# Moving copies, scatters and early weight loads within the step order of a fused attention and mixture-of-experts kernel

## The chip, the cores and the metric

The kernel runs on one core of a Trainium2 chip. The metric is the device time of one execution in microseconds (us). The core's engines each take their own instructions strictly in the order in which the program lists them: TensorE (PE, with its weight loads shown apart as PEld), VectorE (DVE), ScalarE (ACT), GpSimd (POOL), and SyncE (SP), which issues most of the transfers. An instruction that waits holds up everything behind it on its own engine.

## What is computed

Eight batches of eight heads, 576 tokens, 64 channels a head. Each head has a local attention (a band of seven keys) and one on means of four tokens; their sum is the input `x` of a mixture of eight experts with one expert for each token.

```python
q_d, k_d, v_d = (t.reshape(B, H, S // 4, 4, D).mean(axis=3) for t in (q, k, v))
out_up    = np.repeat(softmax(q_d @ k_d.T / 8) @ v_d, 4, axis=2)
out_local = softmax(where(abs(i - j) < 4, q @ k.T / 8, -1e9)) @ v
x         = (out_up + out_local).transpose(0, 2, 1, 3).reshape(4608, 512)
logits    = x @ w_gate + modality_bias[modality_id]
e         = argmax(logits);  g = softmax(logits)[e]
out[t]    = g[t] * (relu(x[t] @ w1[e]) @ w2[e])        # e: the expert of token t
```

## The kernel before

**The order.** The attention handles two heads at once: 32 pairs, n = 0 to 31, four to a batch b. The work of one pair is cut into some fifty small functions, and the table `PHASE` (line 61) gives each a due time in steps: function f of pair n is due at n + PHASE[f], a function of the router (the part that finds each token's expert) for batch b at 4b + PHASE[f]. `build` collects all of them in `calls` with other work that has a due time of its own, sorts the list and calls it (lines 1344 to 1348) under a manual schedule. Within one engine the instructions therefore stand in order of due time. A due time is no time of day: it settles only what stands ahead of what in each engine's queue. One step took some 6 to 8 us, and several pairs are in flight at once. Below, "step 31" is the stretch of due times 31.0 to 32.0.

**One pair.** PE transposes q and k (`tpq`, `tpk`, `tpt`), ACT copies them from PSUM (`qT`, `kT`: the copy of k is two instructions of 64 rows each, a = 0 and a = 1, line 330), DVE makes k's means (`kd`), POOL q's (`qe`, `qd`). PE makes the local scores (`sc0`, `sc1`) and those of the means (`scd`). DVE takes maxima and differences (`lm`, `le`, `dm`), ACT the exponentials (`exp`, `de`), DVE sums and reciprocals (`z`, `zr`), POOL normalises (`nl` for the local part, line 426; `nd` for the means, line 430), DVE transposes the local part (`lt`), PE the other (`pdt`, line 451, which needs `nd`), ACT copies both (`Pw0` to `Pw3`, `PdT`), PE multiplies with v (`avd`, `avl`), and DVE adds the two into `X` (`X0`, `X1`).

**The router**, once a batch. `lg` makes the logits (PE, one step after the batch's last pair has left), `LT0` and `LT1` copy them from PSUM in two halves (ACT, line 535), `lgt` transposes them (PE), `L`, `ch1`, `ex`, `ch2`, `gt` choose the expert (DVE and ACT), `pr` ranks the tokens (PE, line 593), `pl` turns the ranks into slots (DVE), `st0` to `st4` scatter token numbers into a table in memory, one indirect transfer of POOL each (line 642), `R` and `W` transpose and store x.

**The start of the experts.** The counts of the first four batches settle the first expert early. Inside the attention's last steps the kernel reads that expert's token list (`entries`, SP), gathers 512 rows of x (`rows`, line 937, four indirect transfers of POOL), loads the first four of eight chunks of its weights (`wload`, line 851, 512 KB a chunk in four transfers of SP) and splits chunks 0 and 1 in two (`wsplit`: a cast on POOL, line 876, then a subtraction on DVE, line 882). Chunks 2 and 3 are split after the last pair. `load_v` loads half a batch of v. When the last pairs are through, PE begins the first expert's matrix products.

Of the kernel before, what the change touches and what calls it, by code (L numbers as in the profile page):

```python
# [19 lines left out]
B, H, S, D = 8, 8, 576, 64  # L20
# [38 lines left out]


PHASE = {
# [10 lines left out]
}  # L72


# [123 lines left out]
class Attention:  # L198
# [120 lines left out]

    def kT_(s, n, i):  # L320
        g = n % 2
        p = s.t["tp", "t"][:, 1] if i else s.t["tp", "k", n]
        for a in range(2):
            r = slice(64 * a, 64 * a + 64)
            if i:
                t = s.kB[r].rearrange("m g a t -> m g (a t)")[:, :, KT * a + PAD : KT * a + PAD + 512 + 64]
                s.nc.scalar.copy(t[:, 0, 512:], p[r, :64])
                s.nc.scalar.copy(t[:, 1, :64], p[r, 64:])
            else:
                s.nc.scalar.copy(s.kB[r, g, a, PAD + 64 * g : PAD + 64 * g + 512], p[r])  # L330
# [867 lines left out]
def build(tc, q, k, v, mid, w_gate, bias, w1, w2, out):  # L1198
    nc = tc.nc
    with ExitStack() as ctx:  # L1200
# [10 lines left out]
        with ExitStack() as actx:  # L1211
# [7 lines left out]
            at = Attention(tc, actx, ectx, C, ps, q, k, v)  # L1219
# [9 lines left out]
            N = 4 * B  # L1229
# [17 lines left out]
            def call(at, f, *args):  # L1247
                calls.append((at, len(calls), f, args))
# [4 lines left out]
            used = max(P["avl0"], P["avl1"])  # L1253
# [3 lines left out]
            for nm, p in P.items():  # L1257
                f, i = (nm[:-1], int(nm[-1])) if nm[-1].isdigit() and nm not in ("ch1", "ch2") else (nm, 0)
                if f in batch:
                    for b in range(B - 1):  # L1260
                        late_ = {2: 0.05, 0: 0.9, 3: 0.14}.get(i, 0) if f == "st" and b == B - 2 else 0
                        call(4 * b + p + late_, getattr(ro, parts.get(f, f)), b, i)
                else:
                    for n in range(0, N, 2 if f in ("vp", "vc", "tpt") or nm in ("qT1", "kT1", "kd1") else 1):
                        call(n + p, values if f == "X" else getattr(at, parts.get(f, f)), n, i)
            for b in range(B):
                if b + 1 < B:
                    for j in range(2):
                        call(4 * b - 1 + used + 0.3 + 0.8 * j, at.load_v, b + 1, 4 * j)
            for h in range(3, N // 2):  # L1270
                call(2 * h - 5 + last + 0.25, at.load_qk, h // 2, h % 2)

# [54 lines left out]
            t = 4 * (EB - 1) + max(P[x] for x in P if x[:2] == "st") + 0.02  # L1327
# [2 lines left out]
            for u in range(KEARLY):  # L1330
                call(t + 1 + 0.1 * u, expert, u)
            for u in range(KEARLY):
                call(t + 1.5 + 0.1 * u, entries, u)
            for i in range(4):
                call(t + 4.75 + 0.3 * i, rows, 0, i)
            free = N - 1 + max(P["scd"], P["sc0"], P["sc1"]) + 0.02

            w = max(t + 5, 4 * (B - 2) - 1 + used + 1.1 + 0.8)
            for c in range(4):
                call(w - 1.5 + 0.5 * c, wload, c)  # L1340
            for c in range(2):
                for j in range(2):
                    call(w + 1.5 + 0.6 * c + 0.25 * j, wsplit, c)
            calls.sort(key=lambda x: x[:2])
            with tc.manual_schedule():
                for x in calls:
# [22 lines left out]
            b = B - 1  # L1369
# [21 lines left out]
        N, written = len(order), ExitStack()  # L1391
# [199 lines left out]
```

## Time and profile before

| what | us |
|---|---|
| runs shown | 667.71, 671.05, 669.85 |
| median of them | 669.85 |
| profiled execution, its own time | 665.86 |
| its span, first to last instruction | 664.2 |
| PE busy in the span | 624.9 (94 %) |
| DVE, ACT, POOL busy in the span | 444.3, 387.3, 338.8 |

All rows below are from the one profiled execution; their times count from its first instruction. In a timeline row the columns are start, length, engine, line, operation, what is written from what is read, shapes and count, and in brackets how long the engine had been idle and what ended that. The attention fills the first 250 us, the experts the rest.

### The profile page before, as it was taken

How to read it: one execution, taken by the hardware profiler on the slowest of the kernel's cores; microseconds unless marked ns; L12 is line 12 of the kernel's file. 1: busy time of each engine (PE TensorE's matmuls, PEld its weight loads, DVE VectorE, ACT ScalarE, POOL GpSimd, SP SyncE). 2: the span in 40 equal slices, each digit the busy share in tenths (PEclk: the TensorE clock that was granted, in tenths of full speed). 3: DMA queues.
4: the chain of work that ended last, by engine and by line, in shares of the span. 5: the costliest groups of instructions: out<-in, count | busy, mean ns of one | idle time of the engine just before them, and what ended most of it. 6: DMA issues, size and time to landing. Idle time of an engine off the chain costs nothing. (4 is left out here: it accounts for less than half of the span.)

```text
span 664.2 us, 16573 instructions
## 1 busy us (share of the span) xinstructions
PE 624.9 (94%) x6131; PEld 497.9 (75%) x6131; DVE 444.3 (67%) x977; ACT 387.3 (58%) x902; POOL 338.8 (51%) x378
## 2 busy tenths in 40 slices
PE   8898989998998879899999999999999999999996
PEld 5676666766666657688888888888888878889794
DVE  6788898989889985644446773758728966236610
ACT  4888989987898863412354742438324473346610
POOL 6634645627376747143049776397775730141211
PEclk9999999998999998999999999999999999999999
DMA  8999898999999936459003435224351245549400
GB/s 188 208 183 196 142 187 159 195 189 159 177 138 203 145 92 174 130 129 226 28 33 104 107 87 158 55 97 106 95 163 65 86 105 154 163 126 292 141 16 33
DMA packets 168862, 90.24 MB, mean 136 GB/s; under 512 B 131812, under 2 KB 153354, under 8 KB 168778
## 3 DMA queue, kind: packets, MB, share of 16 engines
q1 hardware_dynamic: 160810, 69.96, 50.0%
q0 software_dynamic: 7968, 19.18, 9.3%
q8 instruction: 50, 0.82, 0.6%
q14 instruction: 34, 0.28, 0.2%
HBM read 69.86 MB, written 19.51 MB: 135 GB/s over the span
## 5 line engine op out<-in xcount | busy, mean ns | idle before, releaser
L1059 PE MATMUL l<-V,H 128*128 128x512 f32 x792 | 184.3, 391 | 0.0
L1059 PEld LDWEIGHTS l<-V,H 128*128 128x128 f32 x792 | 147.8, 188 | 30.6
L945 POOL DMA_INDIRECT xg<-xs,m x64 | 74.9, 1170 | 19.2 <-issue 19.2
L426 POOL TENSOR_TENSOR le<-le,zr 128x384 f32<-128x384 f32 x32 | 26.6, 833 | 86.3 <-DVE zr L422 73.2
L1069 POOL DMA_INDIRECT out_dram<-o,tq x24 | 26.8, 1116 | 76.6 <-ACT o L1061 48.2
L442 ACT COPY Pw<-lt 32x288 f32<-32x288 f32 x128 | 54.6, 426 | 3.7 <-DVE er L712 1.2
L1005 PE MATMUL l<-X,H 128*128 128x512 f32 (+1 forms) x240 | 54.0, 376 | 2.2 <-DVE H L1011 2.2
L1061 ACT ACTIVATE o<-l,tq 128x512 f32<-128x512 f32 x24 | 16.5, 688 | 60.5 <-PE l L1059 39.5
L642 POOL DMA_INDIRECT tab<-ig,si x36 | 38.2, 1062 | 23.3 <-DVE mbase L784 17.1
L1005 PEld LDWEIGHTS l<-X,H 128*128 128x128 f32 x240 | 42.0, 190 | 10.7 <-DVE H L1011 2.5
L1162 ACT ACTIVATE H<-o 128x512 fp32r<-128x512 f32 x36 | 22.8, 634 | 37.7 <-DVE o L1184 37.7
L481 PE MATMUL avl<-Pw,vw 128*64 128x96 f32 x768 | 39.7, 252 | 4.6 <-ACT Pw L442 4.6
L481 PEld LDWEIGHTS avl<-Pw,vw 128*64 128x64 f32 x768 | 33.2, 138 | 12.6 <-ACT Pw L442 7.4
L882 DVE TENSOR_TENSOR V<-raw,V 128x1024 fp32r<-128x1024 f32 x22 | 30.9, 1423 | 13.1 <-ACT V L876 13.1
L330 ACT COPY kT<-tp 64x512 f32<-64x512 f32 x64 | 37.0, 579 | 2.5 <-PE tp L294 1.4
L1011 DVE SCALAR_TENSOR_TENSOR H<-l,H 128x512 fp32r<-128x512 f32 x24 | 16.4, 688 | 32.3 <-ACT H L1010 32.0
L1069 POOL DMA_INDIRECT out_dram<-o,tg x10 | 12.0, 1198 | 48.2 <-ACT o L1061 35.9
L412 ACT ACTIVATE de<-scd,dm 128x144 f32<-128x144 f32 x96 | 35.3, 376 | 1.9
L372 PE MATMUL sc<-kT,qT 128*24 128x64 f32 x1536 | 34.5, 223 | 0.9 <-ACT kT L330 0.9
L344 DVE TENSOR_REDUCE kd<-tp 128x128 f32<-128x512 f32 x32 | 21.4, 670 | 17.4 <-ACT kT L330 15.6
L372 PEld LDWEIGHTS sc<-kT,qT 128*24 128x24 f32 x1536 | 24.5, 103 | 10.6 <-issue 4.2
L1010 ACT ACTIVATE H<-l 128x512 fp32r<-128x512 f32 x24 | 14.2, 596 | 31.1 <-PE l L1005 31.1
(281 smaller groups left out, 1463.4 us busy)
## 6 DMA issues: line engine op xcount, KB each, us to landing
raw<-in_moe_w_dram SPq DMA_DIRECT2D x112, 128.0 KB
raw<-in_moe_w_dram SPq DMA_DIRECT2D x28, 512.0 KB
vw<-in_v_dram SPq DMA_DIRECT2D x60, 180.0 KB
qt<-in_q_dram SPq DMA_DIRECT2D x26, 288.0 KB
kt<-in_k_dram SPq DMA_DIRECT2D x26, 288.0 KB
xs<-R SPq DMA_DIRECT2D x56, 128.0 KB
qt<-in_q_dram SPq DMA_DIRECT2D x6, 256.0 KB
kt<-in_k_dram SPq DMA_DIRECT2D x6, 256.0 KB
```

What stands on the lines that cost most here:

```text
L330: s.nc.scalar.copy(s.kB[r, g, a, PAD + 64 * g : PAD + 64 * g + 512], p[r])
L372: s.nc.tensor.matmul(p[32 * j : 32 * j + SUB, 2 * i : 2 * i + 2, :], qT[:, q0 : q0 + SUB], kB[:, :, q0 : q0 + WIN], start=False, stop=(i = ...
L412: s.nc.scalar.activation(x, s.t["scd", n][:, c].rearrange("p (k x) -> p k x", k=NB), AF.Exp, bias=m[:, c : c + 1], accum_out=s.t["z", n][: ...
L426: s.nc.gpsimd.tensor_tensor(e, e, z[:, : 2 * NB].unsqueeze(2).broadcast_to([128, 2 * NB, WIN]), op=ALU.mult)
L442: s.nc.scalar.copy(s.Pw[n % NPW][r, :, j, :SUB], s.t["lt", n][r, :, :SUB])
L481: s.nc.tensor.matmul(p[64 * a : 64 * a + 64, c], vw[:, NB * (4 * (hp // 2) + hp % 2 + 2 * a) + k, :], Pw[:, 2 * k + a], start=True, stop=T ...
L642: i = nc.gpsimd.indirect_dma_start(out=s.tab[:, :], out_offset=bass.IndirectOffsetOnAxis(ap=C.si[:, t : t + 1], axis=0), in_=C.ig[:, t, :] ...
L882: (nc.gpsimd if turn == 4 else nc.vector).tensor_tensor(lo, raw, hi.bitcast(F32), op=ALU.subtract)
L945: s.nc.gpsimd.indirect_dma_start(out=R[l].rearrange("p h (i x) -> p (h i) x", i=4)[:, i, :], out_offset=None, in_=s.xs.rearrange("n (a x) ...
L1005: nc.tensor.matmul(p[:, f % n, :], a[:, fs], x[:, k, :N], start=(k == 0 and i == 0), stop=(k == 3 and i == 2))
L1059: nc.tensor.matmul(p, l, x[:, f % 2, :], start=(f == 0 and i == 0), stop=(f == 7 and i == 2))
L1069: nc.gpsimd.indirect_dma_start(out=s.out[:, :], out_offset=bass.IndirectOffsetOnAxis(ap=T[:, h, 0:1], axis=0), in_=o, in_offset=None, boun ...
```

## The change

No instruction is added or removed. The due times change, and one loop is cut in two.

- `kT` becomes two functions: `kT0` (a = 0, due 0.1900) and `kT2` (a = 1, due 0.2050). The first half of the logits' copy, `LT0`, is due at 0.1923 in the steps that have one, so it now stands between the two copies of k.
- `pr` goes from 7.8428 to 8.1000, `pl` from 7.9316 to 8.1300.
- The scatters go from fractions of a step of 0.00, 0.20, 0.59 and 0.62 to 0.62 and 0.63, behind `qe` of the same step: `st4` 9.0000 to 9.6238, `st2` 8.5946 to 8.6300, `st3` 9.5946 to 9.6300, `st1` 10.2000 to 10.6300. Batch 6's own lateness grows, so that its `st0` goes from 33.52 to 33.74, across `nd` of the last pair (33.60).
- v of the last batch: due 25.45 and 26.86, where it was 26.84 and 27.64.
- The token list is read at 25.30 (was 23.72), and its four gathers are due at 28.64, 29.64, 30.64 and 30.66 (were 26.97 to 27.87).
- The chunks 0 to 3 are asked for at 28.3, 29.3, 30.3 and 31.3 (were 26.94, 27.44, 27.94, 28.44). The split of chunks 0 and 1 moves from 29.94, 30.19, 30.54 and 30.79 to 31.15, 31.40, 31.66 and 31.91 (each cast, then subtraction).

```diff
-    ... "tpt": 0.1888, "kT0": 0.2050, "qT1": 0.5097,
+    ... "tpt": 0.1888, "kT0": 0.1900, "kT2": 0.2050, "qT1": 0.5097,
...
-    "R4": 7.7000, "gt": 7.8318, "pr": 7.8428, "pl": 7.9316, "st4": 9.0000, "W2": 8.5000, "R1": 8.2990, "W0": 9.1000,
-    "st2": 8.5946, "st0": 8.6238, "R2": 9.2990, "st3": 9.5946, "st1": 10.2000, "R3": 10.2990, "W1": 11.1000,
+    "R4": 7.7000, "gt": 7.8318, "pr": 8.1000, "pl": 8.1300, "st4": 9.6238, "W2": 8.5000, "R1": 8.2990, "W0": 9.1000,
+    "st2": 8.6300, "st0": 8.6238, "R2": 9.2990, "st3": 9.6300, "st1": 10.6300, "R3": 10.2990, "W1": 11.1000,
...
     def kT_(s, n, i):
-        p = s.t["tp", "t"][:, 1] if i else s.t["tp", "k", n]
-        for a in range(2):
+        p = s.t["tp", "t"][:, 1] if i == 1 else s.t["tp", "k", n]
+        for a in (0, 1) if i == 1 else (i // 2,):
...
-                        late_ = {2: 0.05, 0: 0.9, 3: 0.14}.get(i, 0) if f == "st" and b == B - 2 else 0
+                        late_ = {2: 0.05, 0: 1.1162, 3: 0.16}.get(i, 0) if f == "st" and b == B - 2 else 0
...
-                        call(4 * b - 1 + used + 0.3 + 0.8 * j, at.load_v, b + 1, 4 * j)
+                        late_ = (1.39, 0.78)[j] if b == B - 2 else 0
+                        call(4 * b - 1 + used + 0.3 + 0.8 * j - late_, at.load_v, b + 1, 4 * j)
...
-                call(t + 1.5 + 0.1 * u, entries, u)
-            for i in range(4):
-                call(t + 4.75 + 0.3 * i, rows, 0, i)
+                call(4 * (B - 2) + 1.3 + 0.01 * u, entries, u)
+            for i, x in enumerate((0.64, 1.64, 2.64, 2.66)):
+                call(4 * (B - 1) + x, rows, 0, i)
...
-            w = max(t + 5, 4 * (B - 2) - 1 + used + 1.1 + 0.8)
             for c in range(4):
-                call(w - 1.5 + 0.5 * c, wload, c)
+                call(4 * (B - 1) + 0.3 + c, wload, c)
             for c in range(2):
                 for j in range(2):
-                    call(w + 1.5 + 0.6 * c + 0.25 * j, wsplit, c)
+                    call(N - 1 + (0.15, 0.66)[c] + 0.25 * j, wsplit, c)
```

## Rows read from the trace of the kernel before

**Rows 1.** By stretch: length, busy PE, PEld, DVE, ACT, POOL; clock, DMA share, GB/s
```profile
220.00:240.00 20.00, 17.39 (x343) 12.72 (x343) 18.22 (x57) 15.66 (x50) 11.07 (x14) 1.00 0.78 148
300.00:320.00 20.00, 20.00 (x92) 16.40 (x90) 7.79 (x17) 5.21 (x8) 6.63 (x7) 1.00 0.76 199
```

**Rows 2.** The waits from 10 to 252 us: who, for whom, us in total, times, longest
```profile
DVE kd L344 <- ACT kT L330: 15.6, 14, 2.2
PE lgt L541 <- ACT LT L535: 6.0, 7, 0.9
PE pdt L451 <- POOL de L430: 5.3, 8, 1.1
ACT LT L535 <- PE lg L528: 5.0, 7, 0.8
ACT qT L318 <- PE tp L298: 4.7, 7, 0.9
PE pr L593 <- DVE X L492: 2.4, 4, 1.1
```

**Rows 3.** Timeline of a step with logits (n = 27), ACT and DVE
```profile
197.25 0.61 ACT L318 ACTIVATE qT<-tp 128x512 f32<-128x512 f32 x1
198.63 0.42 ACT L535 COPY LT<-lg 128x320 f32<-128x320 f32 x1 [0.77 <-PE lg L528]
198.96 1.19 ACT L330 COPY kT<-tp 64x512 f32<-64x512 f32 x2
200.17 0.42 ACT L535 COPY LT<-lg 128x320 f32<-128x320 f32 x1
200.18 0.69 DVE L344 TENSOR_REDUCE kd<-tp 128x128 f32<-128x512 f32 x1 [1.37 <-ACT kT L330]
```

**Rows 4.** Busy time by stretch, as Rows 1, cut at the ends of waits
```profile
188.91:197.86 8.95, 8.77 (x178) 6.53 (x182) 7.93 (x22) 8.78 (x31) 6.51 (x10) 1.00 0.92 144
200.18:214.53 14.35, 12.54 (x253) 9.61 (x253) 13.76 (x47) 12.34 (x40) 8.14 (x11) 1.00 1.07 199
230.28:242.18 11.90, 9.67 (x185) 7.17 (x186) 11.35 (x40) 8.31 (x30) 5.39 (x8) 1.00 0.67 166
239.70:249.22 9.52, 5.89 (x76) 4.22 (x78) 6.98 (x15) 7.25 (x22) 5.94 (x7) 1.00 0.25 55
249.22:252.63 3.41, 3.41 (x23) 2.10 (x19) 2.54 (x5) 1.51 (x4) 3.31 (x3) 0.50 0.26 57
```

**Rows 5.** Timeline, a transpose behind a scatter in a middle step, PE and ACT
```profile
212.17 0.61 PE L451 MATMUL pdt<-ident,de 64*96 64x64 f32 x12 [0.69 <-POOL de L430]
212.93 0.68 ACT L459 COPY PdT<-pdt 96x288 f32<-96x288 f32 x2
```

**Rows 6.** Timeline of steps 29 to 31, early weights on POOL and DVE
```profile
219.78 0.69 ACT L459 COPY PdT<-pdt 96x288 f32<-96x288 f32 x2 [0.56 <-PE tp L298]
220.67 1.23 DVE L882 TENSOR_TENSOR H<-raw,H 128x1024 fp32r<-128x1024 f32 x1 [0.83 <-POOL H L876]
220.79 2.00 POOL L642 DMA_INDIRECT tab<-ig,si  x1 [0.16 <-issue]
...
226.88 1.20 DVE L882 TENSOR_TENSOR H<-raw,H 128x1024 fp32r<-128x1024 f32 x1
...
230.28 0.65 DVE L344 TENSOR_REDUCE kd<-tp 128x128 f32<-128x512 f32 x1
```

**Rows 7.** Timeline of the attention's end (step 33), POOL and PE
```profile
244.31 0.82 POOL L426 TENSOR_TENSOR le<-le,zr 128x384 f32<-128x384 f32 x1 [3.07 <-ACT Pw L442]
245.30 1.01 POOL L642 DMA_INDIRECT tab<-ig,si  x1 [0.16 <-issue]
...
246.34 0.91 POOL L430 TENSOR_TENSOR de<-de,zr 128x432 f32<-128x432 f32 x1
...
247.19 1.04 POOL L876 CAST H<-raw 128x1024 fp32r<-128x1024 f32 x1
...
247.31 0.54 PE L451 MATMUL pdt<-ident,de 64*96 64x64 f32 x12 [1.04 <-POOL de L430]
```

**Rows 8.** Timeline in the experts' part, DVE beside POOL
```profile
348.06 4.56 DVE L882 TENSOR_TENSOR V<-raw,V 128x1024 fp32r<-128x1024 f32 x2
349.12 2.41 POOL L1116 TENSOR_TENSOR raw<-raw,raw 128x1024 f32<-128x1024 f32 x1
```

More of the change, by code (lines that the diff above doesn't have):

```diff
@@ L321, in kT_ @@
         g = n % 2
-        p = s.t["tp", "t"][:, 1] if i else s.t["tp", "k", n]
-        for a in range(2):
+        p = s.t["tp", "t"][:, 1] if i == 1 else s.t["tp", "k", n]
+        for a in (0, 1) if i == 1 else (i // 2,):
             r = slice(64 * a, 64 * a + 64)
-            if i:
+            if i == 1:
                 t = s.kB[r].rearrange("m g a t -> m g (a t)")[:, :, KT * a + PAD : KT * a + PAD + 512 + 64]
```

2 rows, old and new, of the table PHASE are left out of this document.

## The prediction

> **What bounds the kernel.** I read the busy time by stretch first [rows 1]. In the experts' part a 20 us stretch has PE busy for all 20.00: nothing that is moved there shortens it, but all of it starts earlier by whatever the attention before it loses. In the attention's stretch PE (17.39), DVE (18.22) and ACT (15.66) are all nearly full, so no engine's share tells what a wait is worth. The reader should ask of each wait whether the next engine in line was still at work without a break when the late thing arrived. The list of waits [rows 2] gives the candidates, one per batch each: DVE's `kd` for the copy of k (15.6 us over 14, the longest), ACT's `LT` for the logits (5.0 over 7), ACT's `qT` for PE (4.7 over 7), PE's `pdt` for POOL (5.3 over 8), `pr` for DVE (2.4 over 4). To sort them I cut the busy time at the ends of waits [rows 4]. ACT is busy 8.78 of 8.95 us from 188.91 to the logits at 197.86; there ACT sets the pace. From `kd` at 200.18 to 214.53 DVE is busy 13.76 of 14.35, and the rest is gaps of some hundredths between instructions; there DVE does. Between the two lies a short passage [rows 3] in which neither works: `qT` ends at 197.86, ACT idles 0.77 until PE has the logits, copies half of them (198.63), then k twice (198.96, 1.19 for both), and only then `kd` starts, DVE having waited 1.37. That passage is the only place where a moved copy is worth its full length.
>
> **Part A, the copies of k.** With the copies split, the first (half of 1.19, 0.595) fits in ACT's idle of 0.77; over the seven passages the idle is 5.0/7 = 0.71, still enough. `LT0` stays at 198.63, the second copy starts at 198.96 instead of 199.56, `kd` at 199.58 instead of 200.18. The gain is 0.60 a passage. DVE is unbroken behind it, so it keeps the 0.60 up to the next stretch that ACT paces, whose input arrives earlier as well. `LT1` and with it PE's `lgt` (waits 6.0/7 = 0.86) also come 0.60 earlier; behind them is DVE's queue, so this is not counted again. Six passages, n = 7 to 27, give 6 x 0.60 = 3.6. The seventh (n = 31) lies in the end part and is counted there. Bounds: 0.4 each if `LT1` or a late PE takes a third of it (2.4), 0.77 each if the idle goes entirely (4.6).
>
> **Part B, `pr` and `pl` later.** PE no longer stands at `pr` waiting for DVE's `X` to give back a PSUM buffer (0.6 a time), and the transposes behind it, on which `qT` waits 4.7/7 = 0.67, come earlier. But this lies inside the stretch where DVE is unbroken [rows 4]: ACT's earlier `qT` only waits longer later. I take 0. Bounds: 0 and -4.7, if ACT's chain were the one that sets the pace; above nothing I allow 0.4, because `pl` now ends later and the scatters need it, though they are moved behind it by half a step.
>
> **Part C, scatters later.** `nd` no longer stands behind an indirect transfer of 1.01 [rows 7] on POOL, so PE's `pdt` need not wait. But in a middle step [rows 5] PE waited 0.69 and ACT started the copy behind it at 212.93 without any idle of its own: ACT was late anyway. I take 0, with bounds of 0 and -3.9: 5.3 less 1.04 for the last pair, counted below, and 0.4 for the drain. The scatter now stands behind `qe`, where POOL has room (11.07 busy of 20 [rows 1]); the tables are needed only at the experts' start.
>
> **Part D, token list, gathers, v, loads.** SP's queue changes: half of the last v goes ahead of the weights and the four weight chunks are a step apart. None of the four compute engines waits for v or a weight before 252 in [rows 2]'s list, so earlier v is worth nothing, and later weights cost nothing as long as a chunk lands within the step before its split. Chunk 0 is asked at 28.3 for 31.15, chunk 1 at 29.3 for 31.66: over two steps, some 15 us. Three gathers (each some 1.01 by the scatter's row, 2.00 at most [rows 6]) now stand on POOL in steps 28 to 30. POOL's idle in the attention (9 us in 20) covers them; if that cover is gone at `nl`, 1.01 is lost for one of them. I take 0, bounds 0 and +1.
>
> **Part E, the early splits.** In step 29 DVE waited 0.83 for the cast and then spent 1.23 on the subtraction, and ACT idled 0.56 at `PdT` [rows 6]. The sub leaves this place, but I can't see that it caused the 0.56: between 0 and -0.56 I take -0.3. In step 31 the chain is DVE's. Without the 1.20 at 226.88 [rows 6] and with the seventh 0.60 partly in it, `kd` of pair 31 starts at about 229.2 instead of 230.28 (-1.08); then a sub of 1.20 stands ahead of `L`, so that the logits of batch 6 come out +0.14. In step 32 the second sub stands in a stretch where DVE is busy 11.35 of 11.90 [rows 4], so its 1.20 is paid in full: `dm`(31), `nl`(30), `nd`(30) come about +1.36. Against that stands the last pair: `nd`(31) no longer waits for `st0` (1.01 and 0.16 of issue, PE waiting 1.04 for it [rows 7]): -1.17. Net +0.2, with bounds of -1.0 (the sub fits in idle that the earlier `kd` leaves) and +1.4 (the last pair was not on the path).
>
> **Part F, two engines at memory.** The sub of chunk 0, which reads two tiles of SBUF, is now issued when POOL has `nl` and `nd` of pair 29 (0.82 + 0.91 [rows 7]). In the experts' part two subs took 4.56 beside a POOL instruction of 2.41, against 2 x 1.20 alone [rows 8, 6]: 2.16 lost, nearly the whole of the POOL instruction. So the cost lies between 0 (DVE comes first, or POOL is idle) and 0.82 + 0.91 = 1.73. Since POOL's work needs DVE's `zr` and the sub stands behind it, they may overlap only briefly: I take 0.2. The Trainium skill says, in "SBUF — State Buffer", section "Who interferes with whom", that a DVE instruction with two SBUF inputs contends with a GpSimd instruction that reads SBUF and that the one issued second blocks for the whole of the other; the 4.56 agree, and by it alone this term would be 0.82 to 1.73, not 0.2. The same section infers that such an operation leaves GpSimd's descriptor generation alone; the scatter of 2.00 at 220.79 beside the sub of 220.67, against 1.01 without one, speaks against that.
>
> **Part G, the clock.** From 249.22 to 252.63 PE was granted 0.50, that is 1.2 GHz of 2.4, after a stretch of 9.52 us in which it was busy for only 5.89 [rows 4]. All of the 3.41 us is PE work, so it costs 3.41/2 = 1.7. The change alters the idle before it in both directions; it may vanish (-1.7) or come twice (+1.7). I take 0.
>
> **Sum.** -3.6 (A) + 0 + 0 + 0 - 0.3 + 0.2 (E) + 0.2 (F) = -3.5. The profiled execution took 665.86 (span 664.2, 1.7 around it), which is 4.0 below the median of the runs shown, so I subtract the 3.5 from the median: 669.85 - 3.5 = 666.35, about 666.4; the profiled execution's like would be 662.4. The forecast's own range, from the bounds of A (-2.4 to -4.6) and of E and F, is 664.5 to 668.3.
>
> **Rivals.** (1) ACT, not DVE, paces the middle steps, and the waits of B and C count. For it: ACT is busy 12.34 of DVE's 14.35, and half of the batch is ACT's stretch already. Against: DVE has no idle there to give. With B's 4.7 the sum is -8.2, with C's 3.9 as well -12.1; between the two I put -10: 659.8. Chance 0.15. (2) The end eats it: A's 3.6 is earned, but the sub blocks for 1.73 instead of 0.2 and PE, idle longer, gets a second half-clock stretch of 1.7. -3.5 + 1.5 + 1.7 = -0.3: 669.5. For it: the drain is the only stretch where PE already idles 3.6 us and falls to half clock. The same time results if the change doesn't do what it says, the logits being late enough that the first copy just delays `LT0`. Chance 0.25. (3) Slower: POOL's and DVE's early split work stands ahead of the last pairs' chain instead of in idle time. Place: steps 31 and 32. Price: two subs 2.4, blocked 1.73, the cast 1.04 [rows 7] and a gather 1.01 ahead of `nl`, and the half clock that PE's longer idle brings, 1.7: 7.9, less 3.6 and 0.3, so +4.0: 673.9. It decides once the end loses more than the 3.9 earned plus 3.35. Against: before, the same subs and casts stood at steps 29 to 31, not in idle time either. Chance 0.08.
>
> **Chances and range.** The forecast has 0.52. About 0.5%, 3.35 us, is what a measurement of this kernel can tell from no change, so below 666.5 counts as faster: the forecast lies at that edge and gives 0.30 to faster and 0.22 to same; rival 1 gives 0.15 to faster; rival 2 0.22 to same and 0.03 to slower; rival 3 0.07 to slower and 0.01 to same. Faster 0.45, same 0.45, slower 0.10. The range runs from rival 1's middle (660.0, which leaves out some 0.07) to beyond rival 2, 671.0 (which leaves out rival 3 and the little above).
>
> **What would show it.** Right: DVE's wait before `kd` in the logits steps falls from 1.37 to about 0.77, ACT's idle before `LT0` from 0.77 to some 0.17, PE's wait at `lgt` from 0.86 to some 0.26. `pr` and `pdt` cease to be waits, and DVE's unbroken stretch keeps its 14.35 us. In step 31 a DVE sub stands ahead of `L`; in step 33 `nd` follows `nl` on POOL at once. Wrong: a DVE stretch shorter than 14.35 (rival 1), subs longer than 1.3 beside POOL or two stretches at 0.50 (rival 2), the last `dm` over 3 us later against its batch than before (rival 3), or a wait for a weight or v ahead of the experts (part D).

## The result and the profile after

The changed kernel took 677.28 us (median of 20 runs, 672.9 to 681.45) against 670.49 for the kernel before (20 runs). The ratio is 1.0096, with a 95 % interval of 1.0073 to 1.0118: some 6.4 us slower, where 3.5 us faster was forecast. Ratios here and below leave out the few executions over 1.5 % above the fastest of their kernel, so they can differ a little from the quotient of the medians. The profiled execution took 679.0 us, its span is 677.2. The page's line of busy times, in us and share of the span:

```profile
PE 635.2 (94%) x6131; PEld 504.3 (74%) x6131; DVE 445.3 (66%) x977; ACT 390.1 (58%) x902; POOL 339.5 (50%) x378
```

No engine was given more to do. PE shows 635.2 us against 624.9, because in this execution it did more of its work at half clock (part G below); the rest is waiting. Where it arose is read from three stretches of the attention, cut at DVE's maximum of the means (`dm`, line 404) for pairs 7, 27 and 31 and at the experts' first matrix product (line 1005). Below they are called the middle, the end and the drain. The columns are those of [rows 1]. First the changed kernel:

```profile
65.31:216.43 151.12, 134.09 (x2579) 98.99 (x2577) 130.83 (x419) 131.04 (x406) 78.14 (x105) 0.99 0.93 166
216.43:251.76 35.33, 28.33 (x474) 20.23 (x474) 27.08 (x81) 23.84 (x74) 22.07 (x28) 0.90 0.62 127
251.76:263.82 12.06, 10.21 (x92) 7.88 (x92) 8.92 (x18) 8.74 (x25) 8.54 (x9) 0.61 0.30 65
```

Then the kernel before, not from the trace of [rows 1 to 8] but from one taken late in the study (e18 below), for a reason that the experiments give:

```profile
63.62:211.73 148.11, 132.50 (x2580) 98.67 (x2577) 131.45 (x418) 129.63 (x406) 82.70 (x109) 0.99 0.94 175
211.73:241.08 29.35, 25.33 (x498) 18.38 (x485) 26.78 (x82) 23.39 (x74) 19.04 (x24) 1.00 0.82 137
241.08:252.56 11.48, 8.00 (x92) 5.89 (x92) 8.92 (x18) 8.70 (x25) 7.90 (x8) 0.88 0.20 44
```

The changed kernel loses 3.0 in the middle (151.12 against 148.11), 6.0 in the end and 0.6 in the drain; with 1.7 ahead of pair 7 this makes the 11.3 by which its experts start later (263.82 against 252.56). DVE's busy time in the middle is even 0.6 less, so DVE has gaps that it did not have. A second trace of the changed kernel (e5 below) has 147.98, 35.00 and 10.12 in the three stretches. So the loss in the end stands in both; the 3.0 in the middle stands only in the one, against this trace of the kernel before.

**What the gaps are.** Waits of the changed kernel from 60 to 225 us (who, for whom, us in total, times, longest), picked from a longer list: POOL's waits, the longest in both kernels, and PEld's are left out.

```profile
DVE lm L379 <- PE pdt L451: 7.3, 7, 2.6
DVE kd L344 <- ACT kT L330: 6.3, 10, 1.3
PE tp L298 <- ACT PdT L459: 5.5, 10, 1.3
ACT PdT L459 <- PE tp L298: 4.3, 8, 1.5
PE pdt L451 <- DVE kd L340: 3.3, 4, 1.5
```

Lines of the same list of the kernel before (e18):

```profile
DVE kd L344 <- ACT kT L330: 7.7, 10, 1.5
PE lgt L541 <- ACT LT L535: 4.3, 5, 0.9
PE pdt L451 <- POOL de L430: 3.3, 6, 1.1
```

`kd`, the wait that part A was to shorten, did shrink (from 7.7 to 6.3; five passages at 0.60 would be 3.0), and `lgt` and POOL's `nd` have left the upper part of the list, as forecast. But two waits are new, both for PE: 7.3 us of DVE at `lm`, and 4.3 of ACT at `PdT`, which holds PE's next transposes for 5.5. The first does not stand in the list of before at all, the second with 0.6 us, once; neither is in [rows 2]. One such place in the timeline of the changed kernel (columns as in [rows 3]):

```profile
193.76 0.54 PE L372 MATMUL sc<-kT,qT 128*24 128x64 f32 x24
193.87 1.01 POOL L642 DMA_INDIRECT tab<-ig,si  x1 [0.15 <-issue]
194.23 0.54 PE L451 MATMUL pdt<-ident,de 64*96 64x64 f32 x12
195.35 0.36 DVE L379 TENSOR_REDUCE lm<-sc 128x6 f32<-128x192 f32 x1 [1.02 <-PE pdt L451]
195.53 0.69 ACT L459 COPY PdT<-pdt 96x288 f32<-96x288 f32 x2 [0.64 <-PE tp L298]
```

`lm` needs only the scores `sc`, which PE had made by 194.30. It starts at 195.35, 1.05 later, having waited 1.02. The profile names `pdt` because that was PE's last work by then, which `lm` does not read; `PdT` likewise starts 0.76 after the `pdt` that it copies. What stands between is the scatter of 193.87. It is off PE, DVE and ACT, and still what PE's rows show as finished was passed on to DVE only 0.47 after the scatter's end.

### The profile page after: what moved, and what is told of

The parts are those of the page before. It is cut to its first block, busy times and chain, and to the rows that moved or that the text cites. A ratio compares the mean times of both kernels' runs of the same rounds, so it can differ in the third digit from the quotient of the medians.

```text
span 677.2 us, 16576 instructions
## 1 busy us (share of the span) xinstructions
PE 635.2 (94%) x6131; PEld 504.3 (74%) x6131; DVE 445.3 (66%) x977; ACT 390.1 (58%) x902; POOL 339.5 (50%) x378
## 5 line engine op out<-in xcount | busy, mean ns | idle before, releaser
L945 POOL DMA_INDIRECT xg<-xs,m x64 | 76.6, 1197 | 19.2 <-issue 18.6
L882 DVE TENSOR_TENSOR V<-raw,V 128x1024 fp32r<-128x1024 f32 x22 | 35.4, 1624 | 13.4 <-ACT V L876 12.6
L1123 DVE TENSOR_TENSOR G<-X,G 128x1024 fp32r<-128x1024 f32 x15 | 23.3, 1556 | 21.3 <-ACT G L1122 21.1
```

What stands on the lines that cost most here:

```text
L882: (nc.gpsimd if turn == 4 else nc.vector).tensor_tensor(lo, raw, hi.bitcast(F32), op=ALU.subtract)
L945: s.nc.gpsimd.indirect_dma_start(out=R[l].rearrange("p h (i x) -> p (h i) x", i=4)[:, i, :], out_offset=None, in_=s.xs.rearrange("n (a x) ...
```

## Experiments

The parts are those of the prediction: A the copies of k, B `pr` and `pl`, C the scatters, D v, token list and gathers, E weight chunks and splits. Ratios are against the kernel before in the same comparison, with 95 % intervals.

**First comparison: each part alone.** Its kernel before has a median of 667.07.

e1, part A alone:

```diff
-    "kT0": 0.2050,
+    "kT0": 0.1900, "kT2": 0.2050,
-        for a in range(2):
+        for a in (0, 1) if i == 1 else (i // 2,):
```

> The kernel before with part A alone: kT in two functions, LT0 between them; nothing else moves. Theory 1 (the loss comes from the scatters and from the end, A itself pays as forecast): kd starts 0.60 us earlier in six passages with logits, so 3.6 us less, ratio 0.9946. Rival (part A is itself the loss, or is given back within the batch, as the batches of the changed kernel from n = 7 to n = 27 took 1 us longer each on average): ratio 1.000 or above.

Measured 665.15, ratio 0.9981 (0.9959 to 1.0003), less than the 0.9946 expected. The passage goes as worked out (below), but the middle is only 1.9 shorter than in e9, and the median 1.9.

e2, part B alone:

```diff
-    "pr": 7.8428, "pl": 7.9316,
+    "pr": 8.1000, "pl": 8.1300,
```

> The kernel before with part B alone: pr and pl later. Theory 1: no change, ratio 1.000. Rival: pr takes its PSUM buffer at another turn, so that pdt in the steps 4b now waits for kd of tpt (in the changed kernel four times, 3.3 us in all): 3 us more, ratio 1.005. Second rival (the forecast's rival 1): ACT's earlier qT counts, 2.4 to 4.7 us less, ratio 0.993 to 0.996.

Measured 667.73, ratio 1.0002 (0.9984 to 1.0019): nothing, as forecast.

e3, part C alone:

```diff
-    "st4": 9.0000, "st2": 8.5946, "st3": 9.5946, "st1": 10.2000,
+    "st4": 9.6238, "st2": 8.6300, "st3": 9.6300, "st1": 10.6300,
-    late_ = {2: 0.05, 0: 0.9, 3: 0.14}.get(i, 0) ...
+    late_ = {2: 0.05, 0: 1.1162, 3: 0.16}.get(i, 0) ...
```

> The kernel before with part C alone: the scatters later, behind qe. Theory 1: a scatter that stands behind qe holds up what PE has to report while sc and pdt are under way (in the trace after, PE's signals pause for 1.4 us from the start of nearly every scatter, and lm waits for them): 1 to 1.5 us a batch in six batches, 6 to 9 us more, ratio 1.009 to 1.013. Rival (the pauses come from the whole change together or from another part): ratio 0.998 to 1.002.

Measured 666.90, ratio 0.9995 (0.9971 to 1.0018). C seemed innocent.

e4, parts D and E:

```diff
+    late_ = (1.39, 0.78)[j] if b == B - 2 else 0            # v, subtracted from its due time
-    call(t + 4.75 + 0.3 * i, rows, 0, i)
+    call(4 * (B - 1) + x, rows, 0, i)                       # x in (0.64, 1.64, 2.64, 2.66)
-    call(w - 1.5 + 0.5 * c, wload, c)
+    call(4 * (B - 1) + 0.3 + c, wload, c)
-    call(w + 1.5 + 0.6 * c + 0.25 * j, wsplit, c)
+    call(N - 1 + (0.15, 0.66)[c] + 0.25 * j, wsplit, c)
```

> The kernel before with parts D and E alone: v, the token list, the gathers, the weight loads and the two splits at their new due times. Theory 1: the end of the attention takes 6.7 us longer in the changed kernel from dm of pair 27 to dm of pair 31, and gathers and splits are what moved there: 5 to 7 us more, ratio 1.007 to 1.010. Rival (the end only passes on what the scatters lost, and the half clock comes from that): ratio 0.998 to 1.003.

Measured 671.66, ratio 1.0070 (1.0043 to 1.0097). So D and E cost 4.6 here; their end stretch is 31.39 us against 28.66 (e9). Not all of it lies there: in the two traces the experts start only 1.6 apart (252.87 and 251.23), and their part takes 416.40 us against 411.20. That part ran from 411.2 (e9) to 420.9 us (e16) over all traces, and what sets it was not followed up, so a trace's total must not be put down to the attention alone. But A to C alone came to -1.4 in sum (-1.9, +0.7, -0.2), so the parts leave +3.2 where the whole lost 6.4. I therefore repeated the whole beside groups of its parts.

**Second comparison: the whole and groups of parts.** Kernel before 669.99, 2.9 above the first comparison's.

e5, the changed kernel once more, as in the diff of the change.

> The changed kernel once more, with a second trace. Theory 2 (the parts add up): A alone measured 0.9981, B 1.0002, C 0.9995, D with E 1.0070, together 1.0048, and PE's signals run on time beside the scatters, as they did with C alone. Theory 3 (together they cost more than one by one): ratio 1.0096 as first measured, and the second trace shows the pauses of 1.4 us in PE's signals from the start of a scatter, which the trace with C alone did not show, and dm of pair 31 some 10 us later than before.

Measured 675.30, ratio 1.0095 (1.0058 to 1.0131): the result stands.

e6, parts A, B and C together (the diffs of e1, e2 and e3).

> The kernel before with A, B and C, without D and E. Theory 2 (the parts add up): 0.9981 x 1.0002 x 0.9995 = 0.9978. Theory 3 (the scatters behind qe hurt only where pr is late or kd early): the five batches between dm of pair 7 and of pair 27 take 5 us longer as in the trace after, ratio 1.005 or more.

Measured 673.71, ratio 1.0078 (1.0050 to 1.0105). Three parts that alone came to 0.9981, 1.0002 and 0.9995 are now slow together; the middle is 152.99.

e7, part E alone (the last two pairs of lines of e4's diff).

> The kernel before with the four weight chunks asked for a step apart and the two splits in steps 31 and 32; v, token list and gathers stay. If the splits ahead of the last pairs' chain cost what D and E together cost: 4.6 us more, ratio 1.007. If the gathers on POOL are the cost: ratio 0.998 to 1.002.

Measured 675.24, ratio 1.0108 (1.0056 to 1.0161) from six runs, three near 672 and three near 679; the trace is of the first sort. No account of mine gives E so much; why it has two sorts is open.

e8, part D alone (the first lines of e4's diff).

> The kernel before with the early v, the late token list and the gathers in steps 28 to 30; weights and splits stay. If the gathers are the cost: three of them ahead of nl at 1.0 each, and the rows they fetch late for the transposes, 3 to 4.6 us more, ratio 1.005 to 1.007. If the splits are: ratio 0.998 to 1.002.

Measured 672.07, ratio 1.0023 (0.9986 to 1.0060).

**What the traces of the two comparisons tell apart.** I counted in each trace, from the times of PE's semaphore signals, the scatters and gathers between 50 and 262 us during which a PE instruction ended, by the profile, and yet no signal of PE's arrived from 0.1 us after the transfer's start to 0.3 after its end. In the trace of before it is 0 of 39, in e1 to e4 0, 1, 2 and 2 of 37 to 39. In the trace of the changed kernel it is 20 of 33, in e5 to e8 21, 23, 15 and 15 of 34 to 36. So there are two kinds of trace, and each comparison is of one kind: in one, PE's signals pause beside a scatter or gather, in the other they hardly do. The kernels are not what differs. The next runs test that with the kernel before and with C taken out and put in alone.

This count is of records, and the traces of the first kind hold fewer of them altogether: 528 to 544 signals of PE for 573 to 576 instructions that give one (561 to 570 in the other kind), and 786 to 806 of DVE for 922 or 923 (896 to 915). So a signal counted as missing may be a lost record. A second count goes by the times of instructions alone: how often, from 60 to 252 us, did `lm` or `PdT` start over 0.4 us after both its engine was free and the product that it reads had ended. With the scatters at their new times it is 12 to 17 times in the traces with pauses (14 here, 13, 17, 12 and 14 in e5, e6, e14 and e16) and never in those without (e3, e10, e11). At the old times it is 1 to 3 with pauses (e7, e8, e13, e15, e17, e18) and 0 or 1 without.

**Third comparison.** Kernel before 666.75.

e9, the kernel before, one execution.

> The kernel before, unchanged, for a second trace. Theory 4 (the pauses of PE's signals beside a scatter belong to the place where the trace was taken, not to the change: the trace of before and e1 to e4 show none, the trace after and e5 to e8 show them, e7 too, whose attention is that of the kernel before up to step 28): if this trace shows pauses, so do the three others of this comparison, and if not, none does. Theory 3 (the change makes them): none here, pauses in the two with the scatters behind qe.

664.22 us; signals missing at 2 of 39.

e10, the changed kernel.

> The changed kernel. Theory 4: with pauses in the traces 1.0095 as in e5, without them the sum of the parts, 1.005 (A 0.9981, B 1.0002, C 0.9995, D with E 1.0070). Theory 3: 1.0095 either way.

Measured 665.19, ratio 0.9980 (0.9962 to 0.9999), missing at 0 of 39: the same program that was 1 % slower twice is now 0.2 % faster. It is also better than the 1.005 that theory 4 had added up from the parts of the first comparison, which suggests that the pauses are not all that differs between comparisons. The step of above, in e10's timeline:

```profile
185.73 0.54 PE L372 MATMUL sc<-kT,qT 128*24 128x64 f32 x24
186.04 1.01 POOL L642 DMA_INDIRECT tab<-ig,si  x1 [0.15 <-issue]
186.20 0.54 PE L451 MATMUL pdt<-ident,de 64*96 64x64 f32 x12
186.41 0.34 DVE L379 TENSOR_REDUCE lm<-sc 128x6 f32<-128x192 f32 x1
186.94 0.69 ACT L459 COPY PdT<-pdt 96x288 f32<-96x288 f32 x2
```

The order and the scatter's length are the same, but `lm` starts during the scatter, 0.14 after `sc`, and neither DVE nor ACT waits.

e11, part C alone again (e3's diff).

> C alone once more. Theory 4: where the traces show pauses, each of the 24 scatters behind qe falls into sc and pdt, and lm waits for it: 5 to 7 us more, ratio 1.007 to 1.010; where they don't, 0.9995 as in e3. Rival: C is worth nothing anywhere, and what e6 lost comes from A with B.

Measured 663.52, ratio 0.9947 (0.9927 to 0.9967), missing at 0 of 39. The interval lies below that of e3 (0.9971 to 1.0018), again without pauses in either. The clock granted to these six executions was 0.997 on average, against 0.993 for the kernel before; by the lost share of the span, that is up to 2.8 of the 3.5 us.

e12, the changed kernel with the scatters at their old times (A, B, D and E):

```diff
-    "st4": 9.6238, "st2": 8.6300, "st3": 9.6300, "st1": 10.6300,
+    "st4": 9.0000, "st2": 8.5946, "st3": 9.5946, "st1": 10.2000,
-    late_ = {2: 0.05, 0: 1.1162, 3: 0.16}.get(i, 0) ...
+    late_ = {2: 0.05, 0: 0.9, 3: 0.14}.get(i, 0) ...
```

> The changed kernel with the scatters at their places of before: A, B, D and E. Theory 4: where the traces show pauses, better than the whole by 0.7 to 1.0%, ratio 1.000 to 1.003; where they don't, like the whole, 1.005. Rival (D and E are the loss everywhere): 1.005 to 1.010 either way.

Measured 667.38, ratio 0.9994 (0.9971 to 1.0017). Without pauses C costs nothing: alone it is 0.9995 and 0.9947, within the whole 0.9980 against 0.9994.

**Fourth comparison, on the same chip as the third.** Kernel before 673.54, and the traces have pauses: so it is not the chip that has them.

e13, e12's kernel again.

> The changed kernel with the scatters at their places of before: A, B, D and E. Without pauses in the traces (as e12): 0.9994. With pauses, theory 4 (scatters behind qe meet sc and pdt, whose signals lm and PdT wait for; at their old places they meet waits that are there anyway): 2 to 4 us less than the whole, ratio 1.003 to 1.006. Rival (with pauses the place of a scatter doesn't matter): 1.0095 as the whole.

Measured 673.08, ratio 0.9998 (0.9959 to 1.0037); missing at 17 of 39. Against the whole's 1.0095 and 1.0096, taking C out gives back about 6.5 us (some 3 to 10 by the intervals, and across comparisons).

e14, part C alone (e3's diff).

> C alone. Without pauses: between 0.9947 (e11) and 0.9995 (e3). With pauses, theory 4: 3 to 5 us more, ratio 1.005 to 1.008. Rival: 1.000.

Measured 681.45, ratio 1.0117 (1.0060 to 1.0174), missing at 22 of 33. With e11 this is the pair that decides: the same kernel, the same chip, 0.5 % faster without pauses and 1.2 % slower with them. The clock is not the cause of the latter: these executions were granted 0.990 on average, the kernel before 0.989.

e15, part A alone (e1's diff).

> A alone. Without pauses 0.9981 as in e1. With pauses, theory 4: the scatters stand where they stood, so A still brings its 1 to 3 us, ratio 0.995 to 0.999. Rival (a pause anywhere in the batch uses up what A brings): 1.000 or above.

Measured 668.65, ratio 0.9940 (0.9897 to 0.9983). A gains here too.

e16, the changed kernel with token list and gathers at their old times, to see whether gathers one after the other on POOL make the end late:

```diff
-    call(4 * (B - 1) + x, rows, 0, i)
+    call(t + 4.75 + 0.3 * i, rows, 0, i)
```

> The changed kernel with the token list and the gathers at their times of before: A, B, C, the early v and E. In the whole, st1, and two gathers stand in a row on POOL in step 30, and with pauses PE's signals stop for 4.7 us there (dm from pair 29 to pair 30 takes 13.9 us against 8.7). With pauses, theory 4: that stop is gone, 3 to 4 us less than the whole, ratio 1.004 to 1.006. Without pauses: like the whole without (0.998). Rival (the subtraction in step 31, 2.66 beside nl and nd in e10, is what the end costs): like the whole either way, 1.0095 or 0.998.

Measured 681.91, ratio 1.0110 (1.0041 to 1.0179) from six executions. The interval holds both what theory 4 expected and the rival's 1.0095, so the time decides nothing. In the trace the stop is gone as expected: `dm`(29) to `dm`(30) takes 8.85 us against 13.83. But the step before it takes 9.43 against 7.50, and the end stretch is still 33.14.

**Fifth comparison.** Kernel before 670.64, traces with pauses.

e17, parts A and B (the diffs of e1 and e2), as the version to keep.

> A and B without C, D and E: the two parts whose stretch of the middle batches was shortest (142.2 us from dm of pair 7 to dm of pair 27 in the whole without pauses, 146.5 before, 144.6 with A alone), without the scatters' new place and without the splits in steps 31 and 32. Theory 4: 3 to 4.5 us less than before with or without pauses, ratio 0.993 to 0.996. Rival (B needs C, since a scatter ahead of nd takes back what the earlier transposes bring): 0.998 as A alone.

Measured 666.42, ratio 0.9951 (0.9914 to 0.9987): 0.5 % better than the kernel before and, by the two ratios, 1.4 % better than the changed one, with pauses.

e18, the kernel before, one execution.

> The kernel before once more, for a trace. If this comparison has the pauses, this trace shows the kernel before with them: some 15 of 39 indirect transfers with PE's signals held, as in e15, and 147 to 151 us from dm of pair 7 to dm of pair 27 against 146.5. If not, it looks like e9.

668.07 us; missing at 16 of 38. So the kernel before has the pauses as well, and its middle is 148.11 with them against 146.47 without (e9). Why they cost it so little is seen in the same step of e18:

```profile
188.85 0.54 PE L372 MATMUL sc<-kT,qT 128*24 128x64 f32 x24
189.32 0.54 PE L451 MATMUL pdt<-ident,de 64*96 64x64 f32 x12
189.50 0.34 DVE L379 TENSOR_REDUCE lm<-sc 128x6 f32<-128x192 f32 x1
190.03 0.69 ACT L459 COPY PdT<-pdt 96x288 f32<-96x288 f32 x2
190.35 1.00 POOL L642 DMA_INDIRECT tab<-ig,si  x1 [0.15 <-issue]
```

At its old time the scatter is issued when `sc` and `pdt` have already been passed on. The new time, behind `qe`, puts it on the two signals for which DVE and ACT stand ready.

**What is open.** What decides whether a session has the pauses was not found. In the traces that have them fewer DMA completions are recorded too (4922 to 5117 on SyncE's queues against 6069 to 6177); whether that has the same cause, and whether the recording itself has a part in the pauses, was not tried. That PE's signals come late is read from their times beside transfers, from the late starts counted above and from C's price in both conditions. The ends of matrix products in the trace are modelled; the Trainium skill says so too in "Perfetto Trace Analysis", section "Summary: the profiler window per engine type": TensorE's shown end is estimated, and the time its semaphore takes is hidden. Even so, the step at 193.76 speaks for the signal being late and not PE's work. By its rows the four ends that PE signals there are due at 194.30, 194.77 (two) and 195.51. The signals are recorded at 195.33, 195.45, 195.48 and 195.55: the first 1.03 late, the last 0.04 after its row. Had PE itself been a microsecond late, it could not have done in 0.22 us what took 1.07 in e10 (186.31 to 187.38). By what path a transfer holds a signal back is open.

## Why the prediction was wrong, step by step

**Part C is the step that failed.** It took 0, with bounds of 0 and -3.9, because POOL had room behind `qe`. It measured about +6.5 in the condition in which the result was taken. POOL did have room. What I left out was that a transfer has a price for another engine: I asked only who stands behind it on POOL's queue. Without pauses the bounds hold (0.9995 and 0.9947, that is -0.3 and -3.5). With them C is 1.0117 alone, and 6.5 us within the whole. A loss had been excluded without a row that excludes it. A trace with pauses would have shown one; the trace I read was without them. There was a hint: the profiled execution lay at 665.86, 0.6 % below the median of the runs shown, and I noted the gap and simply forecast from the median. The medians of the comparisons now show two groups: 667.07 and 666.75 without pauses, 669.99, 670.64 and 673.54 with them; the 665.86 fits the first, the median of 669.85 the second.

The ratios with pauses can be added up, across comparisons and each good to 2.4 to 3.6 us by the intervals: A with B -3.3 (e17), D with E +3.2 more (e13, against e17), C +6.5 more (the whole, against e13), together the +6.4 of the result. The forecast had -3.6, +0.1 and 0. So C's price comes first, and the end's, put at next to nothing, second.

**Part A, the copies of k: the passage right, the gain less certain.** The passage of [rows 3], n = 27, in the changed kernel:

```profile
203.80 0.58 ACT L330 COPY kT<-tp 64x512 f32<-64x512 f32 x1
204.56 0.43 ACT L535 COPY LT<-lg 128x320 f32<-128x320 f32 x1 [0.18 <-PE lg L528]
205.01 0.58 ACT L330 COPY kT<-tp 64x512 f32<-64x512 f32 x1
205.62 0.43 ACT L535 COPY LT<-lg 128x320 f32<-128x320 f32 x1
205.63 0.69 DVE L344 TENSOR_REDUCE kd<-tp 128x128 f32<-128x512 f32 x1 [0.79 <-ACT kT L330]
```

The first copy fits in ACT's idle, and 0.18 of it is left (0.17 forecast); DVE waits 0.79 (0.77 forecast) instead of 1.37. The 3.6 measured 1.9 (e1; -0.2 to 2.7 by its interval) and 4.0 (e15; 1.1 to 6.9). So the wait fell as worked out, but in e1 the time fell by less than the forecast, and how much of each 0.60 lasts to the end of a batch is not settled.

**Part B: right at 0.** But it is not free of effects: PE's `pdt` now waits for DVE's `kd` of line 340 (3.3 us over 4, in the list above), a PSUM buffer's turn, in place of the wait for POOL's `nd`.

**The drain: right, and a little more.** The last pair's `nd` no longer stands behind `st0`. In e18:

```profile
245.54 0.82 POOL L426 TENSOR_TENSOR le<-le,zr 128x384 f32<-128x384 f32 x1 [3.06 <-ACT Pw L442]
246.53 1.01 POOL L642 DMA_INDIRECT tab<-ig,si  x1 [0.16 <-issue]
247.57 0.92 POOL L430 TENSOR_TENSOR de<-de,zr 128x432 f32<-128x432 f32 x1
```

and in e10:

```profile
243.34 0.83 POOL L426 TENSOR_TENSOR le<-le,zr 128x384 f32<-128x384 f32 x1 [3.00 <-ACT Pw L442]
244.14 0.90 POOL L430 TENSOR_TENSOR de<-de,zr 128x432 f32<-128x432 f32 x1
```

1.17 was forecast. Without pauses the drain took 9.85 in e10 and e11 against 11.67 in e9, so it was 1.8. Part of that may be the clock: 0.87 in e9's drain, 1.00 in the other two.

**Parts D, E and F, the end: mis-sized.** These are the stretches without pauses, e9 and then e10:

```profile
64.43:210.90 146.47, 130.75 (x2580) 97.48 (x2578) 131.53 (x418) 129.29 (x406) 82.83 (x109) 1.00 0.96 177
210.90:239.56 28.66, 24.36 (x498) 18.00 (x486) 26.48 (x81) 23.54 (x74) 19.07 (x24) 1.00 0.85 132
239.56:251.23 11.67, 8.17 (x92) 6.11 (x92) 8.93 (x18) 8.74 (x25) 8.03 (x8) 0.87 0.20 43
```

```profile
65.24:207.44 142.20, 131.38 (x2579) 97.48 (x2577) 129.72 (x419) 129.79 (x406) 78.08 (x105) 1.00 0.93 170
207.44:238.87 31.43, 25.83 (x474) 18.64 (x474) 28.98 (x82) 23.38 (x74) 23.00 (x28) 0.95 0.91 178
238.87:248.72 9.85, 7.31 (x99) 5.07 (x95) 8.28 (x18) 8.54 (x25) 6.53 (x7) 1.00 0.23 51
```

The middle gains 4.3 (3.0 was forecast for the five passages in it), the end loses 2.8, the drain gains 1.8; with 0.8 lost ahead of pair 7 the experts start 2.5 earlier. The whole measured -0.2 %: this is rival 2, "the end eats it", which had put the whole within 0.1 % of no change. The experts' part after it is 1.4 longer (661.3 - 248.72 against 662.4 - 251.23); I didn't follow that up. By steps, from one `dm` to the next, the end of e9 is 6.18, 7.11, 8.69 and 6.68 us and that of e10 6.17, 6.13, 10.59 and 8.54. The second, rid of its sub, gained 1.0 (0.3 was taken); the fourth, with the second sub, lost 1.9 (1.2 was taken); the third, with the first sub, lost 1.9, where I had taken +0.14 and part F's 0.2. Part F is there:

```profile
226.06 0.84 POOL L426 TENSOR_TENSOR le<-le,zr 128x384 f32<-128x384 f32 x1
226.18 2.66 DVE L882 TENSOR_TENSOR H<-raw,H 128x1024 fp32r<-128x1024 f32 x1
226.85 0.90 POOL L430 TENSOR_TENSOR de<-de,zr 128x432 f32<-128x432 f32 x1
227.72 1.65 POOL L350 TENSOR_TENSOR qe<-qT 128x288 f32<-128x288 f32 x1
...
233.23 0.18 PE L593 MATMUL pr<-oh,tri 128*128 128x32 bf16 x1 [3.48 <-DVE X L492]
```

The sub began 0.12 after `nl` and took 2.66 instead of 1.20: 1.46 lost, within the bounds of 0 to 1.73 but far from the 0.2 taken. The logits of batch 6 wait behind it, and PE stood 3.48 at `pr` (1.32 in e9). POOL's `qe` behind it took 1.65, against 0.67 in e18. This agrees with the rule of the Trainium skill that the prediction quoted ("SBUF — State Buffer", section "Who interferes with whom"): 0.82 to 1.73 by it, 1.46 measured. But e10 is the only trace in which this happened. In the trace of the result both early subs took 1.22, so there F cost nothing. Nor is F the whole of the end's loss: in e4 and e12, both without pauses, the two early subs take 1.22 to 1.43, and the end is still 31.39 and 32.41. In e4 its four steps are 7.05, 6.80, 9.46 and 8.08. The fourth is 1.4 above e9's, which is the second sub. The first and third, 0.9 and 0.8 above, hold one and two of the gathers that part D put at nothing. That the gathers cause it is not shown, and rows speak against it: the third also holds the first sub of 1.22, e7, with the subs but no gather moved, has 9.79 there (with pauses, 8.81 in e18), and in e10 the first step holds a gather and takes 6.17, no more than in e9. Part D's sign of being wrong, a wait for a weight, also came: the cast of chunk 1 waited 1.42 for its load in e10 and 1.23 in e13. What it cost was not measured.

**With pauses, the end is worse.** The changed kernel in step 30, POOL, then DVE and ACT:

```profile
230.43 1.04 POOL L642 DMA_INDIRECT tab<-ig,si  x1 [0.15 <-issue]
231.78 1.04 POOL L937 DMA_INDIRECT xg<-xs,tg  x1 [0.30 <-issue]
233.13 1.01 POOL L937 DMA_INDIRECT xg<-xs,tg  x1 [0.31 <-issue]
...
235.04 0.46 DVE L492 TENSOR_TENSOR X<-avl,Od 128x288 f32<-128x288 f32 x1 [2.44 <-PE sc L372]
235.92 0.69 ACT L459 COPY PdT<-pdt 96x288 f32<-96x288 f32 x2 [3.72 <-PE pdt L451]
```

Three transfers follow each other within 3.7 us; DVE stands 2.44 and ACT 3.72. From `dm`(29) to `dm`(30) it is 13.83 us against 8.81 in e18; the second run of the changed kernel with pauses (e5) has 13.87. Without the gathers there (e16) the step takes 8.85, without the scatter (e13) 10.86: it takes the three together.

**Part G, the clock: more in the trace shown, little over all executions.** Two stretches of the changed kernel, columns as before (the clock is the third number from the end):

```profile
234.01:240.84 6.83, 6.14 (x65) 4.27 (x65) 3.34 (x9) 3.55 (x8) 4.62 (x7) 0.50 0.94 232
254.49:264.73 10.24, 9.40 (x76) 7.46 (x75) 7.03 (x13) 6.15 (x15) 8.13 (x7) 0.50 0.25 51
```

Both are at 0.50, that is 1.2 GHz of 2.4. In the 8.01 us ahead of the first PE was busy for 5.97, in the 10.49 ahead of the second for 7.10. Before there was one such stretch at the attention's end, of 3.41 [rows 4] (and another of 3.41 at 153.6, in the middle, which the prediction did not count). PE's work in the two is 6.14 + 9.40 against 3.41. If all of it is on the path, half of the 12.1 more, about 6.1 us, is what the clock took of this one execution; the bound was 1.7. But this execution is not a typical one: its clock over the whole span, 0.980, is the lowest of the 20, whose mean is 0.989. In the second comparison the changed kernel was granted 0.990 on average and the kernel before 0.992. By the lost share of the span that is some 1.2 us more, so over all executions the clock is a small part of the loss and within the bound.

**The rivals.** Rival 3 had the right side and a near price (673.9), but another mechanism: the split work ahead of the last pairs is in the end's loss without pauses (2.8), which the drain and the middle outweigh there. Rival 1 (ACT sets the pace, -10) did not come: the middle gained 4.3 at most, with C (e10) and, in the other condition, without it (e13, 143.80 against 148.11). Whether the waits for `nd` in it were worth nothing, as taken, is not settled: without pauses and without C (e12) the middle is 146.19, but with 6.83 us of it at half clock, where e10 has none.

## What to carry to other kernels

Before a trace is used for a forecast, its own time should be set against the runs': here 0.6 % between them meant another condition, in which another order of the code is the better one, and two kernels should be compared only by runs and traces of one session. An indirect transfer that is moved should be bounded above zero too, and not on its own queue alone: look which signals of other engines are due in the microsecond beside it, and put it where they have already been passed on. A version that does not lose in either condition (here A: 0.9981 and 0.9940; A with B was measured with pauses only) is worth more than one that is best in one of them (C alone: 0.9947 and 1.0117).

## What the runs showed of the hardware that was not expected

- PE's completion signals can come late beside a scatter or gather of POOL of 1.0 us, not before some 1.4 us after its start (the step at 193.76 above). In some sessions no signal is recorded beside 15 to 23 of 33 to 39 transfers, in others beside 0 to 2; the same chip showed both. In that step PE's work was not late with it: its fourth signal came 0.04 after its row.
- One kernel's ratio can change sides with it: C alone 0.9947 (0.9927 to 0.9967) and 1.0117 (1.0060 to 1.0174).
- In e10 a DVE sub with two SBUF inputs, issued 0.12 us after POOL's normalisation `nl`, took 2.66 instead of 1.20, and POOL's `qe`, begun while the sub ran, 1.65 instead of 0.67.
